# Attention and two dense layers on one core: equal blocks of tokens, and the first batch's attention moved ahead of the first product

## The chip, the cores and the metric

One core of a Trainium2 chip runs the whole program. The metric is the time of the execution on the device in microseconds (us); the median of three runs of the kernel before is 1441.01 us (1440.41 to 1442.49). TensorE (PE) multiplies, VectorE (DVE), ScalarE (ACT) and GpSimd (POOL) do the elementwise work, and SyncE (SP) issues every DMA.

## What is computed

```
k_p, v_p = mean of k, v over groups of 8 keys               # 8 batches, 8 heads, 576 tokens, 64 wide; 72 pooled keys
x = softmax(q @ k_p.T / 8) @ v_p                            # 4608 tokens x 512
h = x @ w_in;   g = where(h > 0, h, exp(min(h, 0)) - 1)     # 512 -> 2048
x1 = g @ w_out                                              # 2048 -> 512
h2 = x1 @ w_in2;  solu = h2 * softmax(h2)                   # 512 -> 1024
out = layernorm(solu) * g_ln @ w_out2                       # 1024 -> 512
```

The weights come as 64-bit floats, everything else as 32-bit floats.

## The kernel before

**Numbers.** Each product is done as three matmuls in a reduced 32-bit type: an operand is split into a high part (a cast, on ACT) and a low part (the rest, on DVE or POOL), and high x high, low x high and high x low are summed. So every first product of 128 columns of weights with a block is 12 matmuls (`m_h1`, L459) and every second one 12 more (`m_o1`, L492).

**Attention** works in units of a batch and a pair of heads: `att_setup` pools k and v, `att_S` makes scores, maxima, differences and exponentials, `att_soft` normalizes, `att_T` transposes, `att_V` multiplies by the pooled values and `att_x` writes the high and low parts of x (`xh`, `xl`). After the first batch a unit is four steps of `att_half`.

**Blocks.** The tokens are cut into blocks of 320, 256, seven of 512 and one of 448 (`sizes`). The first batch of 576 tokens is the first two blocks: its attention is split into units of 320 tokens and units of 256. The units of 320 are done in `startup`, before the first product, in an order written out by hand; those of 256 lie in block 0. The first phase then goes over slots (block `j`, 128 columns `f` of the 2048): the first product, exp, the ELU (`m_elu`, `m_glo`), the split of 128 rows of `w_out`, the second product of the slot before. A credit decides how many steps of attention go into each half slot: `need[j + 1]` is the step by which the next block's x is done.

**Weights.** In block 0 each slot also loads and converts two chunks of 128 (`conv_load`, `conv`): one pass of ACT (L400) and three bit operations of DVE (L402, L404, L406) over 1024 columns, then the split (`conv_split`, with the low part on POOL at L423). The raw 64-bit chunks, the blocks of x and the x1 on its way out share six buffers, tag `x`; wide weights and the loads of the first batch share eight, tag `w`. In the last block five slots convert the second phase's weights in the same way.

**Second phase.** 36 tiles of 128 tokens: h2, softmax and layernorm, transposes, product with `w_out2`.

**Order.** Each engine runs its own queue in order. Queues are filled by a scheduler that ranks instructions by the program's order and a model of their costs; `startup` alone is recorded as written. A tile's buffer is reused when its last reader is done, and the issue of a load into it waits on SP for that, with all later loads behind it.

Of the kernel before, what the change touches and what calls it, by code (L numbers as in the profile page):

```python
# [18 lines left out]
def kernel(  # L19
# [25 lines left out]
    SPLIT = 320  # L45
    NEXP = 12
    HS = S // 2
# [40 lines left out]

    st = {}

    def has_setup(i):
        return i == 0 or units[i][:2] != units[i - 1][:2]

    def att_load(i, what="kqv"):
        b, p, u = units[i]
        c, co = (slice(0, S), 0) if b else (slice(SPLIT, S), 0) if u else (slice(0, 384), 0)
        if i < NP:
            if ("kv", p) not in st:
                kv = sb.tile([P, 4, 512], F32, name=f"kv{i}", tag="w", bufs=8)
                kv = kv.rearrange("p a f -> p (a f)")  # L100
                n = S + P * POOL
                st["kv", p] = (kv[:, 0:S], kv[0:SK, S:n].rearrange("s (c t) -> s c t", t=POOL), kv[:, n:n + 384])
            k_t, v_t, q_t = st["kv", p]
        else:
            if i >= 2 * NP:
                k_t = sb.tile([P, S], F32, name=f"k{i}", tag="k", bufs=1)
                v_t = sb.tile([SK, P, POOL], F32, name=f"v{i}", tag="v", bufs=1)
                st["ld", i] = (k_t, v_t)
            else:
                what = "q"  # L110
            q_t = sb.tile([P, S], F32, name=f"q{i}", tag="q")
            q_t = q_t[:, c]
        if "k" in what:
            nc.sync.dma_start(out=k_t, in_=kT[b, p])
        if "q" in what:
            nc.sync.dma_start(out=q_t, in_=qT[b, p, :, c])
# [4 lines left out]
    nset = [0]  # L121
# [8 lines left out]
    def att_setup(i, what="kv"):  # L130
        b, p, u = units[i]
        early = i < NP
        if early:
            k_t, v_t, _ = st["kv", p]
# [6 lines left out]
        elif i < 2 * NP:  # L141
            return
        else:
            k_t, v_t = st.pop(("ld", i))
            kp = kpbd[nset[0] % 2]
            nset[0] += 1
# [16 lines left out]
    def att_S0(i):  # L163

        if i % 2 == 0:
            st["s0"] = ps.tile([P, 2, 512], F32, name=f"s{i}", tag="A")
        s = st["s0"]
        kp, vt = st["kp", 0, units[i][1]]
        q_t = st.pop(("q", i))
        for t in range(3):  # L170
            nc.tensor.matmul(
                s[:, i % 2, t * 2 * SK:(t + 1) * 2 * SK], q_t[:, t * P:(t + 1) * P], kp, start=True, stop=True
            )

    def att_soft0(i0):

        s = st["s0"]
        n = 6 * SK
        sv = s[:, :, 0:n].rearrange("p a (g k) -> p a g k", k=SK)
        if i0 == 0:  # L180
            st["es"] = xtile("es", F32).rearrange("p a f -> p (a f)")
        es = st["es"][:, i0 * n:(i0 + 2) * n].rearrange("p (a g k) -> p a g k", a=2, k=SK)
        mx = sb.tile([P, 2, 6, 1], F32, name=f"mx{i0}", tag="mx", bufs=4)
        sm = sb.tile([P, 2, 6, 1], F32, name=f"sm{i0}", tag="mx", bufs=4)
        nc.vector.tensor_reduce(mx[:, :, :, 0], sv, axis=AX, op=ALU.max)
        yield
        nc.vector.tensor_tensor(es, sv, mx.to_broadcast([P, 2, 6, SK]), op=ALU.subtract)
        yield
        nc.scalar.activation(es, es, AF.Exp, scale=1.0 / (8 * POOL))
        yield  # L190
        nc.vector.tensor_reduce(sm[:, :, :, 0], es, axis=AX, op=ALU.add)
        nc.vector.tensor_scalar(sm, sm, 1e-9, None, op0=ALU.add)
        nc.vector.reciprocal(sm, sm)
        yield
        nc.vector.tensor_tensor(es, es, sm.to_broadcast([P, 2, 6, SK]), op=ALU.mult)
        for a in range(2):
            st["a", i0 + a] = (es[:, a], st["kp", 0, units[i0 + a][1]][1], 6, None)
        yield

    def att_S(i):  # L200
        b, p, u = units[i]
        kp, vt = st["kp", b, p]
        q_t = st.pop(("q", i))
        tiles = QT[u]
        n = 2 * len(tiles)
        es = sb.tile([P, 10, SK], F32, name=f"es{i}", tag="es")
        mx = sb.tile([P, 10], F32, name=f"mx{i}", tag="mx", bufs=4)
        sm = None
        for t0 in range(0, len(tiles), 3):
            ts = tiles[t0:t0 + 3]  # L210
            m = 2 * len(ts)
            s = ps.tile([P, 512], F32, name=f"s{i}_{t0}", tag="C")
# [4 lines left out]
            sv = s[:, 0:m * SK].rearrange("p (a k) -> p a k", k=SK)  # L217
# [563 lines left out]
```

## Time and profile before

| | |
|---|---|
| median of the runs | 1441.01 us |
| the profiled execution | 1445.27 us |
| its span | 1443.1 us |
| PE busy | 1384.8 us (96%) |
| DVE, ACT, POOL busy | 796.6, 609.1, 333.0 us |
| bytes moved by DMA | 83.06 MB |

The span runs from the first to the last instruction of the program. A matmul's busy time overlaps that of the next one, so PE's progress is read from the time between starts, and busy shares from the union. "PEclk" in the tables of stretches is the granted share of PE's full clock. In rows of a timeline the bracket tells how long the engine stood idle before and what ended the wait.

### The profile page before, as it was taken

The numbers are of one execution on the slowest core, as the hardware profiler recorded it, in microseconds if no ns is written. First come the engines' busy times: TensorE is split into PE (matmuls) and PEld (weight loads), VectorE is DVE, ScalarE is ACT, GpSimd is POOL, SyncE is SP. The second block draws the span as 40 slices with busy tenths as digits, with TensorE's granted clock in tenths as the row PEclk, the third lists the DMA queues.
The fourth block names the chain that finished last, engine by engine and source line by source line (L and its number), as shares of the span: only waits on it lengthen the run. The fifth ranks groups of instructions, "written<-read, shape, count | busy, mean of one in ns | idle before, by whom it ended". The sixth has DMA issues, their size and how long they took to land.

```text
span 1443.1 us, 17607 instructions
## 1 busy us (share of the span) xinstructions
PE 1384.8 (96%) x6752; PEld 1134.5 (79%) x6752; DVE 796.6 (55%) x1357; ACT 609.1 (42%) x1260; POOL 333.0 (23%) x269
## 2 busy tenths in 40 slices
PE   4878999999999999999999999999999999999998
PEld 2667888787887878878788788778888888888886
DVE  5898665555465554555554333675744444455442
ACT  2555654444344444444443433444533333333332
POOL 4454433223232232322323222331000000000000
PEclk9998999999999999999999999999999999999999
DMA  6543221121121111111010010512201110110000
GB/s 211 170 158 129 68 64 42 33 64 33 33 70 34 40 56 34 42 63 42 17 46 1 8 51 0 175 59 84 74 22 51 52 52 22 52 52 22 23 22 30
DMA packets 41876, 83.06 MB, mean 58 GB/s; under 512 B 4160, under 2 KB 14912, under 8 KB 41792
## 3 DMA queue, kind: packets, MB, share of 16 engines
q1 hardware_dynamic: 41792, 81.94, 17.4%
q8 instruction: 53, 0.87, 0.2%
q14 instruction: 31, 0.25, 0.1%
HBM read 63.05 MB, written 18.87 MB: 57 GB/s over the span
## 4 chain that ended last, share of the span: by engine, by line
PE 86%; DVE 7%; ACT 2%; issue 2%; POOL 1%; DMA 1%; SPq 0%; ACTq 0%; DVEq 0%; POOLq 0%
PE h L459 25%; PE o L492 25%; PE po L577 14%; PE h L533 13%; PE s L214 2%; PE pv L300 2%; PE pt L562 2%; PE pt L261 2%; DVE cv L406 1%; DVE cv L404 1%; DMA kv<-in_v 1%; PE pv L310 0%; DVE e L470 0%; DVE wo L404 0%; PE pr L266 0%
## 5 line engine op out<-in xcount | busy, mean ns | idle before, releaser
L442 POOL TENSOR_TENSOR wol<-wo,woh 128x512 fp32r<-128x512 f32 x160 | 223.5, 1397 | 536.5 <-ACT woh L441 534.5
L459 PE MATMUL h<-xh,wh 128*128 128x512 f32 (+3 forms) x640 | 251.2, 392 | 3.4 <-DVE e L471 2.2
L459 PE MATMUL h<-xh,wl 128*128 128x512 f32 (+3 forms) x640 | 239.6, 374 | 5.8 <-POOL wl L423 5.8
L492 PE MATMUL o<-gh,woh 128*128 128x512 f32 (+3 forms) x640 | 240.7, 376 | 3.6 <-ACT gh L473 3.6
L459 PE MATMUL h<-xl,wh 128*128 128x512 f32 (+3 forms) x640 | 240.2, 375 | 0.0
L492 PE MATMUL o<-gh,wol 128*128 128x512 f32 (+3 forms) x640 | 237.8, 372 | 0.0
L470 DVE TENSOR_SCALAR e<-e 128x512 f32<-128x512 f32 (+3 forms) x160 | 72.9, 456 | 259.1 <-ACT e L464 258.8
L577 PE MATMUL po<-wh,dhl 128*128 128x512 f32 x576 | 187.3, 396 | 1.6 <-ACT dhl L565 1.6
L464 ACT ACTIVATE e<-h 128x512 f32<-128x512 f32 (+3 forms) x160 | 88.8, 555 | 229.5 <-PE h L459 227.9
L473 ACT CAST gh<-e 128x512 fp32r<-128x512 f32 (+3 forms) x160 | 92.6, 578 | 149.8 <-DVE e L471 149.8
L459 PEld LDWEIGHTS h<-xh,wh 128*128 128x128 f32 x640 | 123.0, 192 | 33.7 <-issue 12.9
L492 PEld LDWEIGHTS o<-gh,woh 128*128 128x128 f32 x640 | 122.5, 191 | 24.6 <-ACT gh L473 4.9
L459 PEld LDWEIGHTS h<-xh,wl 128*128 128x128 f32 x640 | 123.1, 192 | 23.7 <-POOL wl L423 7.4
L492 PEld LDWEIGHTS o<-gh,wol 128*128 128x128 f32 x640 | 122.6, 192 | 20.5
L459 PEld LDWEIGHTS h<-xl,wh 128*128 128x128 f32 x640 | 122.6, 192 | 20.1
L577 PEld LDWEIGHTS po<-wh,dhl 128*128 128x128 f32 x576 | 107.9, 188 | 28.5 <-ACT dhl L565 2.1
L441 ACT CAST woh<-wo 128x512 fp32r<-128x512 f32 x160 | 99.2, 621 | 66.8 <-PE o L492 59.4
L533 PE MATMUL h<-wh,x1h 128*128 128x512 f32 x288 | 115.2, 400 | 0.8 <-DVE x1s L504 0.5
L577 PE MATMUL po<-wl,dhl 128*128 128x512 f32 x288 | 113.8, 395 | 0.0
L552 POOL TENSOR_TENSOR sc<-sc,mhalf 128x1 f32<-128x1 f32 x36 | 19.7, 548 | 407.0 <-DVE sc L551 407.0
L542 ACT ACTIVATE e<-h,sc 128x1024 f32<-128x1024 f32 x36 | 40.2, 1116 | 173.6 <-DVE sc L541 173.6
L533 PE MATMUL h<-wl,x1h 128*128 128x512 f32 x288 | 112.7, 391 | 0.0
(586 smaller groups left out, 2200.1 us busy)
## 6 DMA issues: line engine op xcount, KB each, us to landing
raw<-in_w SPq DMA_DIRECT2D x48, 512.0 KB
x1r<-x1d SPq DMA_DIRECT2D x9, 1024.0 KB
out<-ot SPq DMA_DIRECT2D x36, 256.0 KB
k<-in_k SPq DMA_DIRECT2D x28, 288.0 KB
v<-in_v SPq DMA_DIRECT2D x28, 288.0 KB
q<-in_q SPq DMA_DIRECT2D x28, 288.0 KB
x1d<-x1s SPq DMA_DIRECT2D x7, 1024.0 KB
kv<-in_k SPq DMA_DIRECT2D x4, 288.0 KB
```

Source lines behind the costliest of these rows:

```text
L214: nc.tensor.matmul(s[:, t * 2 * SK:(t + 1) * 2 * SK], q_t[:, o:o + P], kp, start=True, stop=True)
L261: nc.tensor.transpose(pt[0:SK, t * P:(t + 1) * P], es[:, 2 * t + h, :], ident)
L441: nc.scalar.copy(oh, t[:, f % 4, :])
L442: nc.gpsimd.tensor_tensor(ol, t[:, f % 4, :], oh.bitcast(F32), op=ALU.subtract)
L459: nc.tensor.matmul(h[:, 0:n], a[g][:, kk, fo:fo + P], x[j][:, kk, 0:n], start=(i == 0), stop=(i == 3 * KDM - 1))
L464: nc.scalar.activation(e[:, 0:n], h[:, 0:n], AF.Exp)
L470: nc.vector.tensor_scalar(e[:, 0:n], e[:, 0:n], 1.0, 1.0, op0=ALU.min, op1=ALU.subtract)
L473: nc.scalar.copy(gh[:, 0:n], e[:, 0:n])
L492: nc.tensor.matmul(acc, a[:, dm * P:(dm + 1) * P], x[:, 0:n], start=(f == 0 and m == 0), stop=(f == NF - 1 and m == 2))
L533: nc.tensor.matmul(h[:, g, :], a[c][:, kk, o:o + P], w[g][:, kk, :], start=(m == 0), stop=(m == 3 * KDM - 1))
L542: nc.scalar.activation(e, hv, AF.Exp, bias=sc[:, 0:1], accum_out=sc[:, 1:2])
L577: nc.tensor.matmul(po, a[:, c, :], w[c // 4][:, c % 4, :], start=(m == 0), stop=(m == 3 * NC2 - 1))
```

## The change

Blocks are nine of 512 tokens. Units are whole: a batch and a pair, 576 tokens. The four units of the first batch are done in `startup`, with scores and values in the double banks (tag `A`) and the product with the reciprocals on DVE; their k and q lie in `w` buffers, their v in two `wo` buffers. `att_V` cuts the values where a block ends (512 and 64 tokens, 448 and 128, ...), not in halves of 288. The 128 tokens of batch 1 that belong to block 2 are kept in a tile `late` and split in the second slot of block 1 (`att_late`). k and v of unit 4 are pooled ahead of the loop, and block 0 takes its steps of attention (batch 1) at the rate of the other blocks, not at 0.75 a half slot.

```diff
-    sizes = [SPLIT, S - SPLIT]
-    while sum(sizes) < NT:
-        sizes.append(min(512, NT - sum(sizes)))
-    starts = [sum(sizes[:j]) for j in range(len(sizes))]
-    NBLK = len(sizes)
-
-    units = [(0, p, 0) for p in range(NP)] + [(0, p, 1) for p in range(NP)]
-
-    units += [(b, p, 2) for b in range(1, NB) for p in range(NP)]
+    NBLK = NT // 512
+    sizes = [512] * NBLK
+    starts = [512 * j for j in range(NBLK)]
+    units = [(b, p) for b in range(NB) for p in range(NP)]
     NU = len(units)
-    QT = {0: (0, P, 2 * P), 1: (0, P), 2: (0, P, 2 * P, 3 * P, S - P)}
+    QT = (0, P, 2 * P, 3 * P, S - P)
...
+        eng = nc.vector if i < NP else nc.gpsimd
+        eng.tensor_tensor(es, es, bc(sm, NG), op=ALU.mult)
...
+        j = b * S // 512
+        n = 512 * (j + 1) - b * S
+        st["pv", i] = []
+        for o, w, blk, at in ((0, n, j, b * S - 512 * j), (n, S - n, j + 1, 0)):
+            pv = next(banks)
+            for h in range(2):
+                d = slice(64 * h, 64 * h + 64)
+                nc.tensor.matmul(pv[d, 0:w], vt[:, d], a[:, h, o:o + w], start=True, stop=True)
+            st["pv", i].append((pv[:, 0:w], blk, slice(at, at + w)))
...
+            if blk == 2 and units[i][0] == 1:
+
+                if "late" not in st:
+                    st["late"] = sb.tile([P, 4, 2 * S - 1024], F32, name="late", tag="late", bufs=1)
+                nc.scalar.copy(st["late"][:, p, :], pv)
+                continue
...
+        K(0)
+        S_(0)
+        K(1)
+        S_(1)
+        M(0)
+        K(2)
+        M(1)
+        S_(2)
+        K(3)
+        att_soft(0)
+        T(0)
+        M(2)
+        S_(3)
+        att_soft(1)
+        T(1)
+        M(3)
+        V(0)
         next(ci)
+        att_soft(2)
+        T(2)
+        V(1)
+        att_x(0)
...
+        for i in range(NP):
+            att_load(i, "kq")
+        att_load(0, "v")
+        att_load(1, "v")
         conv_load(("i", 0))
+        att_load(2, "v")
+        att_load(3, "v")
         conv_load(("o", 0))
         startup()
...
+    att_setup(NP)
 
     slots = [(j, f) for j in range(NBLK) for f in range(NF)]
     for si, (j, f) in enumerate(slots):
         if f == 0:
             credit = 0.0
-            rate = 0.75 if j == 0 else max(need[j + 1] - step if j + 1 < NBLK else 0, 0) / (2.0 * NF)
+            rate = max(need[j + 1] - step if j + 1 < NBLK else 0, 0) / (2.0 * NF)
```

In `startup`, K, S_, M, V and T are the pooling of k, the scores, the maxima with the exponential, the pooling of v with the value product, and the transposes of a pair.

On DVE in the startup, before, the softmax of two pairs (`es`) alternates with the conversion of the first weights (`cv`):

```order
L191 TENSOR_REDUCE sm_129<-es 128x12
L192 TENSOR_SCALAR sm_129<-sm_129 128x12
L193 RECIPROCAL sm_129<-sm_129 128x12
L195 TENSOR_TENSOR es<-es,sm_129 128x864
L404 SCALAR_TENSOR_TENSOR cv<-raw,cv 128x1024
L185 TENSOR_REDUCE mx_162<-s_136 128x12
L187 TENSOR_TENSOR es<-s_136,mx_162 128x864
L406 SCALAR_TENSOR_TENSOR cv<-raw,cv 128x1024
```

On DVE at the same place now, `es_131`, `es_154` and `es_193` are the pairs 1, 2 and 3 of the first batch, and `k_346`, `k_352`, `k_399` the loads of k of units 4, 5 and 6:

```order
L200 TENSOR_TENSOR es_131<-es_131,sm_194 128x720
L134 TENSOR_REDUCE kr_359<-k_346 128x72
L175 TENSOR_REDUCE mx_216<-at_187 128x6
L184 TENSOR_TENSOR es_193<-at_187,mx_216 128x432
L175 TENSOR_REDUCE mx_216<-at_187 128x4
L184 TENSOR_TENSOR es_193<-at_187,mx_216 128x288
L196 TENSOR_REDUCE sm_234<-es_154 128x10
L197 TENSOR_SCALAR sm_234<-sm_234 128x10
L198 RECIPROCAL sm_234<-sm_234 128x10
L134 TENSOR_REDUCE kr_542<-k_352 128x72
L200 TENSOR_TENSOR es_154<-es_154,sm_234 128x720
L134 TENSOR_REDUCE kr_740<-k_399 128x72
```

The conversion moved behind these rows, and three reductions of batch 1's k moved in among the softmax of pairs 1 to 3.

On ACT, before, around the first exponential of the ELU (`e<-h`), one pass over raw weights (L400) stands ahead of the last cast of x:

```order
L286 COPY a_v<-pt_1_248 72x320
L400 ACTIVATE wo<-raw 128x1024
L321 CAST xh_194<-pv_254 128x320
L464 ACTIVATE e<-h_268 128x320
L441 CAST woh<-wo 128x512 x2
```

On ACT at the same place now, where `xh_266` is block 0's x and `xh_270` block 1's:

```order
L247 CAST xh_266<-at_328 128x512
L144 ACTIVATE vt_358<-vr_363 72x128
L341 ACTIVATE cv<-raw 128x1024
L247 CAST xh_270<-at_328 128x64
L341 ACTIVATE wo<-raw 128x1024
L405 ACTIVATE e<-h_366 128x512
```

The two passes over raw weights (now L341) moved between the last cast of block 0's x and the first exponential.

On POOL now, the low part of the first weights (`wl`) stands ahead of the adds over v of pair 3 (the last three of `v_92`); before it stood ahead of those of pairs 2 and 3:

```order
L113 TENSOR_TENSOR v_92<-v_92 72x128x4
L113 TENSOR_TENSOR v_92<-v_92 72x128x2
L115 TENSOR_TENSOR vr_302<-v_92 72x128
L364 TENSOR_TENSOR wl<-cv,wh 128x4x128 x2
L113 TENSOR_TENSOR v_92<-v_92 72x128x4
L113 TENSOR_TENSOR v_92<-v_92 72x128x2
L115 TENSOR_TENSOR vr_323<-v_92 72x128
```

Only pair 3 still follows the weights there, and its adds begin when the casts of the first weights are done.

## Rows read from the trace of the kernel before

**Rows 1.** Busy time by stage: stretch, its length, each engine, clock, DMA share, GB/s
```profile
0.00:42.80 42.80, 21.32 (x68) 11.93 (x68) 24.07 (x35) 13.67 (x26) 15.71 (x23) 1.00 0.63 190
42.80:142.40 99.60, 79.35 (x438) 70.29 (x438) 93.55 (x123) 56.54 (x155) 51.24 (x35) 0.90 0.49 160
142.40:207.00 64.60, 62.90 (x488) 56.84 (x486) 43.00 (x91) 40.42 (x139) 26.97 (x21) 1.00 0.21 62
207.00:308.40 101.40, 101.40 (x498) 81.66 (x497) 56.02 (x98) 44.24 (x91) 27.85 (x21) 1.00 0.13 41
308.40:411.10 102.70, 102.70 (x498) 82.41 (x496) 55.88 (x98) 44.66 (x91) 27.82 (x21) 1.00 0.15 45
820.70:908.90 88.20, 88.20 (x386) 72.20 (x385) 30.43 (x53) 30.38 (x51) 20.42 (x16) 1.00 0.07 24
908.90:1005.60 96.70, 87.74 (x397) 76.74 (x395) 68.73 (x83) 45.43 (x74) 33.69 (x20) 0.95 0.31 109
1005.60:1443.10 437.50, 431.60 (x2016) 354.00 (x2016) 209.03 (x398) 158.92 (x287) 19.74 (x36) 1.00 0.11 41
```
**Rows 2.** DVE's busy time in block 0 at L402, L404, L406, L470, L471, L480
```profile
42.80:142.40 99.60, 11.32 (x13) 0.90 0.49 160
...
42.80:142.40 99.60, 21.19 (x13) 0.90 0.49 160
...
42.80:142.40 99.60, 19.64 (x15) 0.90 0.49 160
...
42.80:142.40 99.60, 8.58 (x16) 0.90 0.49 160
...
42.80:142.40 99.60, 7.09 (x15) 0.90 0.49 160
...
42.80:142.40 99.60, 14.57 (x15) 0.90 0.49 160
```
**Rows 3.** Timeline of the startup: start, length, engine, line, operation, wait before it
```profile
1.24 0.57 SPq L114 DMA_DIRECT2D kv<-in_k  x1
...
4.57 0.75 DVE L150 TENSOR_REDUCE kr<-kv 128x72 f32<-128x576 f32 x1 [3.10 <-DMA kv<-in_k]
...
5.36 0.19 DVE L152 COPY kz<-kr 64x72 f32<-64x72 f32 x1
...
10.60 1.06 DVE L185 TENSOR_REDUCE mx<-s 128x12 f32<-128x864 f32 x1
...
17.91 2.65 POOL L126 TENSOR_TENSOR kv<-kv 72x512 f32<-72x512 f32 x2 [16.28 <-DMA kv<-in_v]
...
18.04 2.05 DVE L195 TENSOR_TENSOR es<-es,sm 128x864 f32<-128x864 f32 x1
...
23.62 1.29 DVE L406 SCALAR_TENSOR_TENSOR cv<-raw,cv 128x1024 uint32<-128x1024 uint32 x1
...
31.61 1.27 DVE L195 TENSOR_TENSOR es<-es,sm 128x864 f32<-128x864 f32 x1
```
**Rows 4.** Group of L471 at 512 columns: busy us, mean ns, idle before
```profile
L471 DVE TENSOR_TENSOR e<-e,h 128x512 f32<-128x512 f32 x112 | 77.0, 688 | 3.1
```
**Rows 5.** Timeline around the first products and of one weight load
```profile
42.50 0.42 ACT L321 CAST xh<-pv 128x320 fp32r<-128x320 f32 x1 [1.76 <-PE pv L310]
...
49.82 0.42 PE L492 MATMUL o<-gh,woh 128*128 128x320 f32 x1
...
95.27 0.81 SPq L384 DMA_DIRECT2D raw<-in_w  x2
...
100.97 1.12 ACT L400 ACTIVATE wo<-raw 128x1024 f32<-128x1024 f32 x1
```
**Rows 6.** Block 9: DVE at L402; one group of matmuls on the chain
```profile
908.90:1005.60 96.70, 7.42 (x7) 0.95 0.31 109
...
991.55 2.44 PE h L459 x12
```
**Rows 7.** Chain of waits: the first twelve matmuls of block 0
```profile
43.25 3.21 PE h L459 x12
```

More of the change, by code (lines that the diff above doesn't have):

```diff
@@ L161, in att_setup @@
         st["kp", b, p] = (kp, vt)
[L163 to L168, printed above, removed]
-        q_t = st.pop(("q", i))
[L170 to L212, printed above, removed]
+    def bc(x, m):
+        return x.rearrange("p (a o) -> p a o", o=1).to_broadcast([P, m, SK])
@@ L213, in att_S, with att_scores @@
+    def att_scores(i, banks):
+        kp, vt = st["kp", units[i][0], units[i][1]]
+        q_t = st.pop(("q", i))
+        st["sv", i] = []
+        for t0 in (0, 3):
+            s = next(banks)
+            ts = QT[t0:t0 + 3]
             for t, o in enumerate(ts):
@@ L235, in att_S, with att_exp @@
-        if i >= NEXP:
-            nc.scalar.activation(es[:, 0:n, :], es[:, 0:n, :], AF.Exp, scale=1.0 / (8 * POOL))
-        st["a", i] = (es, vt, n, sm)
+                nc.vector.tensor_tensor(es[:, g0:g0 + m, :], sv, bc(mxs, m), op=ALU.subtract)
+    def att_exp(i):
+        es, vt = st["a", i]
+        if ("sm", i) not in st:
+            nc.scalar.activation(es, es, AF.Exp, scale=1.0 / (8 * POOL))
     def att_soft(i):
-        es, vt, n, sm = st["a", i]
+        es, vt = st["a", i]
+        sm = st.pop(("sm", i), None)
@@ L273, in att_T @@
+            nc.vector.tensor_reduce(sm, es, axis=AX, op=ALU.add)
+        nc.vector.tensor_scalar(sm, sm, 1e-9, None, op0=ALU.add)
+        nc.vector.reciprocal(sm, sm)
+        eng = nc.vector if i < NP else nc.gpsimd
+        eng.tensor_tensor(es, es, bc(sm, NG), op=ALU.mult)
+    def att_T(i, h):
+        es, vt = st["a", i]
+        if h == 0:
+            st["aT", i] = sb.tile([SK, 2, S], F32, name=f"a{i}", tag="a")
+        a = st["aT", i]
         pt = ps.tile([P, 512], F32, name=f"pt{i}_{h}", tag="C")
-        for t in range(n // 2):
+        for t in range(4):
@@ L313, in att_x @@
[L313 to L322 removed]
+        nc.scalar.copy(a[:, h, 0:4 * P], pt[0:SK, :])
@@ new lines, in att_T, with att_V @@
+        if h == 1:
+            pr = ps.tile([P, 512], F32, name=f"pr{i}", tag="C")
+            for g in range(2):
+                nc.tensor.transpose(pr[0:SK, g * P:(g + 1) * P], es[:, 8 + g, :], ident)
+            lo = 5 * P - S
+            nc.scalar.copy(
+                a[:, :, 4 * P:S], pr[0:SK, 0:2 * P].rearrange("s (g t) -> s g t", g=2)[:, :, lo:P]
+            )
+    def att_V(i, banks):
+        b, p = units[i]
+        es, vt = st.pop(("a", i))
+        a = st.pop(("aT", i))
+        j = b * S // 512
[7 more added lines that the diff above has]
+            st["pv", i].append((pv[:, 0:w], blk, slice(at, at + w)))
@@ L324, with att_late, single, double @@
+    def att_late():
+        t = st.pop("late")
+        th, tl = (x[:, :, 0:2 * S - 1024] for x in xblk(2))
+        nc.scalar.copy(th, t)
+        nc.vector.tensor_tensor(tl, t, th.bitcast(F32), op=ALU.subtract)
+    def single():
+        while True:
+            yield ps.tile([P, 512], F32, name="at", tag="C")
+    def double():
+        t = ps.tile([P, 2, 512], F32, name="at2", tag="A")
+        yield t[:, 0]
+        yield t[:, 1]
     NSTEP = 4 * NU + 3
@@ L329, in att_half @@
         while nload[0] < min(NU, n // 4 + 3):
-            if nload[0] < 2 * NP or has_setup(nload[0]):
-                att_load(nload[0])
+            att_load(nload[0])
             nload[0] += 1
         i, r = divmod(n, 4)
-        whole = i > 0 and units[i - 1][2] == 2
+        before = NP <= i - 1
         if r == 0:
-            if i >= 1 and i - 1 >= NP and not whole:
-                att_T(i - 1, 1)
             if i < NU:
-                att_S(i)
+                for _ in att_scores(i, single()):
+                    pass
+                att_max(i)
+                att_exp(i)
         elif r == 1:
@@ L342, in att_half @@
                 att_soft(i)
-            if whole:
+            if before:
                 att_T(i - 1, 1)
         elif r == 2:
-            if i >= 1 and i - 1 >= NP:
-                att_V(i - 1)
-            if i + 1 < NU and has_setup(i + 1):
+            if before:
+                att_V(i - 1, single())
+                att_x(i - 1)
+            if i + 1 < NU:
                 att_setup(i + 1)
@@ L356 @@
     for j in range(NBLK):
-        end = starts[j] + sizes[j]
-        i = max(m for m in range(NU) if units[m][0] * S + SPLIT * (units[m][2] == 1) < end)
+        i = ((starts[j] + sizes[j] - 1) // S) * NP + NP - 1
         need.append(min(NSTEP, 4 * i + 7))
```

214 lines of the change are left out of this document (62 added, 152 removed).

## The prediction

> **What bounds the kernel now.** I read the busy table by stage first: the cuts are where the first product of each block of tokens begins. [rows 1] has, in order, the startup, block 0 (320 tokens), block 1 (256), block 2 and block 3 (512 each, with a batch of attention beside them), block 8 (512, no attention), block 9 (448) and the second phase. PE is busy in every microsecond of blocks 2 and 3 and of block 8, and in 431.6 of the 437.5 us of the second phase; nothing the change does off PE can show there. The time that can be won or lost lies in three rows: the startup (42.8 us, PE mostly without work), block 0 (99.6 us for 320 tokens, PE 79.35 at a granted clock of 0.90) and block 9 (96.7 us for 448 tokens at 0.95). Block 1 is near its own limit (62.9 of 64.6).
>
> Then I asked who is full in block 0: DVE, 93.55 of 99.6 us [rows 1]. By line [rows 2], 52 us of it is the three bit operations L402, L404, L406 that turn the 64-bit weights into floats, about 3.75 us for each pair of rows (11.3/13 + 21.2/13 + 19.6/15, which is 3.8), and 30 us is the ELU (L470, L471, L480). A conversion costs the same for a block of 320 tokens as for one of 512. So block 0 is a stretch whose length DVE sets, with too little matmul work laid beside it.
>
> **The change, part by part.** Blocks 2 to 7 with their batches of attention, 207.0 to 820.7, are 613.7 us; in the new kernel these are blocks 1 to 6, the same instructions but for the widths of the value products. Block 8 becomes block 7 (88.2) and the second phase stays (437.5). Together 1139.4 us on both sides. What differs is T, the time at which the second block starts (before: block 2, at 207.0, 576 tokens done; now: block 1, 512 tokens done), and L, the last block (96.7 before). 207.0 + 96.7 + 1139.4 is the 1443.1 us span.
>
> *Startup.* Each of four pairs now has five score tiles, not three. On DVE a pair costs: k reduced 0.75 and two copies of 0.2; maximum, difference and sum over 720 columns, 0.9 each (864 columns take 1.06); reciprocal and small ones 0.4; the product with the reciprocals 1.06 to 1.7 (864 columns took 1.27 alone and 2.05 beside a POOL add); the low parts of x, 512 and 64 columns, 0.9 (L471 takes 0.69 for 512 columns; the rest for the small one) [rows 3, 4]. That is 6.2 to 6.9, four times 27.5 at the upper end. The first conversion adds 3.4, and the scheduler has pulled in three reductions of k of batch 1 (2.2) and the first maxima of it (1.5): 34.6 us of DVE work. To it come waits: 4.6 until the first k is there. The reduction of k of unit 4 stands in DVE's queue ahead of the maxima of unit 3, and its load is the 18th on SP, behind 5.6 MB; 3.3 MB had landed when v came at 17.9 [rows 3], so I put it at 25 to 31, and DVE gets there at about 22: 3.5 us taken, up to 8. The next two k go through one buffer, each load issued only when the reduction before it has ended, and a k took 3.3 us from issue to use (1.24 to 4.57) [rows 3]: 3 us each. Sum 4.6 + 34.6 + 3.5 + 6 = 48.7: the first weights are converted at 48.7, before at 24.9 (23.62 + 1.29) [rows 3].
>
> From there: two casts of 512 columns (1.1, as one pass of 1024 at L400), two low parts on POOL (2.6, as two adds) and behind them, now, the three adds over v of pair 3 (3.5; two took 2.65), scale, value product and cast of x (2): about 9 us, so x of block 0 is whole at 57.5; before, its last cast began at 42.50 [rows 3, 5]. Between that cast and the first matmul of the second product there were 7.3 us (42.50 to 49.82); now two passes of 1.12 for the next weights stand on ACT ahead of the first exponential, so 10 us: 67.5 against 49.8 [rows 5]. The startup costs about 18 us.
>
> *Block 0.* Fifteen slots follow, each a first and a second product of 24 matmuls. PE: 88.2/16 = 5.5 us a slot without attention, and (102.7 - 88.2)/16 = 0.9 with it: 6.4 [rows 1]. DVE: 93.55 us before; 192 more columns cost L471 and L480 0.21 each (687 ns at 512 against 473) and L470 nothing, 16 times 0.42 = 6.7; attention is four whole units instead of four halves and three setups ahead, which I cost at nothing because three k reductions have left for the startup; 100.3 over 16 slots, less the share of one conversion already made, is 6.1 a slot [rows 1, 2, 4]. So the two engines are now level, where before PE was busy for 5.0 us a slot, part of it at half clock, and DVE for 5.8. If one hides the other wholly, a slot is 6.5; DVE's fill of block 0 (94%) gives 6.5 from its side too. Two level engines with two buffers between them don't hide each other wholly. The other bound is block 9, where the same conversions stand beside PE-bound work: a group of 12 matmuls there takes 2.44 us, 32 groups 78, the block 96.7, and 7 conversions began in it: 2.7 us for each [rows 1, 6]. Thirteen of these on fifteen slots make 8.8. I take 7.1, near the row of block 0, since there no weight buffer has to come free as in the last block. T = 67.5 + 15 x 7.1 = 174. The bounds are 165 and 199.
>
> The loads of weights: only two of the six x buffers are left to them, as before from the middle of block 0 on. A load issued at 95.27 was in use at 100.97 [rows 5], and a buffer comes round every two slots, 14 us: hidden. If slots fell under 6 us it would not be.
>
> *Last block.* 512 columns: 88.2 of pure work against 78, and each slot is 0.66 longer, which takes something off every stall: of 18.7 us lost I keep 15. L = 103, between 98 and 107.
>
> *Small ones.* The low parts of x in two pieces a unit instead of three save DVE and ACT work in blocks where PE is full: nothing. The copy of 128 late columns and their split in block 1 (0.7 us on each engine) likewise. If their cover fails they cost under 1 us.
>
> Sum: 174 + 103 + 1139.4 = 1416.4 against 1443.1, so 26.7 us less. The profiled execution took 1445.27 us, 4.3 over the median of 1441.01; taking the difference off the median gives 1414.
>
> **Two rules of the Trainium skill.** In block 0 the granted clock is 0.90, and the first 12 matmuls of 320 columns took 3.21 us, after a startup of scattered work; at block 8's pace per column they would take 1.7 [rows 1, 7]. TensorE: Matmul & The Clock Gate (Part 1) says that PE drops to half its clock after idling and regains it once busy; that speaks against the new hole in front of the second product, and by it an estimate is up to 5 us more for the first 24 matmuls. The trace agrees with the direction; I count none of it, since the slots that follow leave PE less idle than before.
>
> The product with the reciprocals took 2.05 us beside POOL and 1.27 alone [rows 3]. SBUF — State Buffer (Who interferes with whom) says that a DVE operation with two SBUF inputs waits out a GpSimd one that reads SBUF; by that each of the four new ones on DVE could lose a whole POOL add of 1.3 (2.65 for two), 5 us together, where my sum has 2.6 at most. The 0.78 of the row agrees with the kind, not the size.
>
> **Rivals.**
> *A conversion costs PE as much as in the last block* (2.7 us each). For: the mechanism, a DVE queue in which three bit operations stand before the next ELU, is the same, and DVE is fuller. Against: there ACT also waited for weight buffers. T = 199, total 1441.4 span, 1439 by the median: no change to a trifle faster.
>
> *DVE and PE take turns.* One mechanism: in each slot the 3.75 us of a conversion add to PE's 6.4 instead of lying beside it. T = 67.5 + 15 x 10.1 = 219, total 1459: slower by 18. It turns to a loss when a slot is over 8.9 us ((207.0 + 96.7 - 103 - 67.5)/15). Against: in block 0 of before, DVE was never stopped for long, so it ran ahead of PE.
>
> *The startup is longer than 67.5*: the load of k for unit 4 late by 8, the next two by 5 each, the first slots at the low clock. 13 to 15 us more, 1428.
>
> *Everything overlaps*: slots of 6.5 and L = 98, 1400.
>
> *The change doesn't take the slack it aims at*, because loads of weights come too late with two buffers: the slot would be the round trip of 5.7 + 1.1 + 3.75 + what DVE has queued, 12 to 14 for two slots, so 6 to 7: no price of its own.
>
> **How the numbers follow.** The forecast, slots of 6.8 to 7.8 and the startup within 6 us, holds 0.55 (1408 to 1426); everything overlaps 0.13; longer startup 0.17; conversions as in the last block 0.07; turns 0.08. A change of 0.2%, 3 us, is what the measurement can tell. Faster 0.87, within 0.2% 0.05, slower 0.08. The range runs from 1401 to 1434.
>
> **What would show it.** The first product of block 0 begins at 49 to 52 and the second near 67; block 1's first product at 165 to 185; DVE and PE both over 85% busy between; granted clock of that stretch over 0.95; six blocks of 102.7 after it, one of 88.2, the last at 98 to 107. A second product later than 75, or slots over 8, make the forecast wrong; so does DVE idle in block 0 for weights that haven't landed.

## The result, and the profile after

The changed kernel takes 1415.99 us (median of 4 runs, 1414.27 to 1419.41) where the kernel before took 1441.24 beside it (4 runs). The ratio is 0.983, with an interval of 0.981 to 0.985: 25 us faster. The forecast was 1414, between 1401 and 1434.

The busy table by stage, of the changed kernel, answers to [rows 1]: stretch, its length, busy time of PE, weight loads, DVE, ACT and POOL, granted clock, share of the DMA engines, GB/s.

```profile
0.00:46.20 46.20, 25.48 (x114) 18.40 (x114) 31.52 (x59) 15.03 (x34) 8.41 (x18) 0.74 0.59 170
46.20:61.20 15.00, 9.02 (x32) 5.58 (x32) 10.53 (x15) 9.62 (x34) 4.76 (x5) 0.79 0.37 122
61.20:174.80 113.60, 102.46 (x461) 77.16 (x461) 107.76 (x125) 66.10 (x164) 58.21 (x36) 0.95 0.47 155
174.80:277.50 102.70, 102.70 (x498) 82.36 (x496) 55.90 (x94) 44.18 (x88) 27.77 (x21) 1.00 0.16 45
277.50:380.30 102.80, 102.80 (x499) 82.44 (x497) 55.61 (x94) 44.19 (x87) 27.89 (x21) 1.00 0.15 45
790.10:878.40 88.30, 88.30 (x387) 72.24 (x386) 30.34 (x52) 30.39 (x50) 20.46 (x16) 1.00 0.07 24
878.40:982.00 103.60, 95.94 (x397) 75.85 (x395) 70.55 (x83) 47.80 (x74) 33.99 (x20) 0.97 0.29 102
982.00:1413.90 431.90, 425.98 (x2016) 353.94 (x2016) 209.08 (x398) 158.88 (x287) 19.73 (x36) 1.00 0.12 42
```

Block 0 begins with its first product at 46.2 and ends at 174.8; its second product begins at 61.2. From there PE and DVE are both nearly full, DVE more so. Six blocks of 512 follow, of which the table has two, then the one without attention, the last one and the second phase. Side by side, in us of the span:

| | before | forecast | after |
|---|---|---|---|
| first second-product begins | 49.8 | 67.5 | 61.2 |
| its 15 slots | | 7.1 each | 7.57 each |
| second block of 512 begins (T) | 207.0 | 174 | 174.8 |
| six blocks with attention | 613.7 | 613.7 | 615.3 |
| block without | 88.2 | 88.2 | 88.3 |
| last block (L) | 96.7 | 103 | 103.6 |
| second phase | 437.5 | 437.5 | 431.9 |
| span | 1443.1 | 1416.4 | 1413.9 |

The order of work gave 32.2 us at T and cost 6.9 in the last block. The 5.6 us of the second phase were in no step of mine.

DVE's lines of block 0 in the changed kernel, which answer to [rows 2]: L343, L345, L347 (bit operations), L411, L412 (ELU) and L421 (low part, gl_).

```profile
46.20:174.80 128.60, 16.61 (x15) 0.93 0.46 151
...
46.20:174.80 128.60, 23.76 (x15) 0.93 0.46 151
...
46.20:174.80 128.60, 21.34 (x15) 0.93 0.46 151
...
46.20:174.80 128.60, 8.28 (x16) 0.93 0.46 151
...
46.20:174.80 128.60, 10.87 (x16) 0.93 0.46 151
...
46.20:174.80 128.60, 19.61 (x16) 0.93 0.46 151
```

These are means of 1.11, 1.58, 1.42, 0.52, 0.68 and 1.23 us. The timeline of the first microseconds shows what lies in them: the same operations are short when POOL is at rest and can be long when it is not (start, length, engine, line, operation, wait before it).

```profile
54.76 0.69 DVE L343 TENSOR_SCALAR cv<-cv 128x1024 uint32<-128x1024 uint32 x1 [0.54 <-ACT cv L341]
...
64.81 0.67 DVE L412 TENSOR_TENSOR e<-e,h 128x512 f32<-128x512 f32 x1
...
66.16 1.84 DVE L421 TENSOR_TENSOR gl__463<-e,gh 128x512 fp32r<-128x512 f32 x1 [0.56 <-ACT gh L414]
...
67.93 1.88 DVE L343 TENSOR_SCALAR wo<-wo 128x1024 uint32<-128x1024 uint32 x1
...
61.25 3.72 POOL L383 TENSOR_TENSOR wol<-wo,woh 128x512 fp32r<-128x512 f32 x2 [10.06 <-ACT woh L382]
...
64.93 2.52 POOL L364 TENSOR_TENSOR wl<-cv,wh 128x512 fp32r<-128x512 f32 x2
...
67.41 1.84 POOL L200 TENSOR_TENSOR es<-es,sm 128x720 f32<-128x720 f32 x1
```

L343 takes 0.69 at 54.76 with POOL idle and 1.88 at 67.93 beside an operation of POOL that ends at 69.25, 0.56 us before it does. L412, whose second input is in PSUM, stays at 0.67.

The chain of waits from 46 to 175 in the changed kernel, some of its longer pieces (start, length, what):

```profile
67.93 1.89 DVE wo L343
...
76.19 1.77 DVE gl__527 L421
...
95.85 2.17 DVE wo L345
...
127.07 2.20 DVE wo L345
...
142.44 2.22 DVE wo L347
...
154.62 2.97 PE h L400 x12
158.03 2.77 PE o L433 x12
```

Until 150 most of its long pieces are DVE's, and long ones of their kind; only then is it PE, at full pace, to the end of the block.

### The profile page after: what moved, and what is told of

Its sections match the earlier page's. It is cut to its first block, busy times and chain, and to the rows that moved or that the text cites. A ratio compares the mean times of both kernels' runs of the same rounds, so it can differ in the third digit from the quotient of the medians.

```text
span 1413.9 us, 16571 instructions
## 1 busy us (share of the span) xinstructions
PE 1362.5 (96%) x6368; PEld 1095.4 (77%) x6368; DVE 786.6 (56%) x1280; ACT 588.6 (42%) x1149; POOL 310.8 (22%) x249
## 4 chain that ended last, share of the span: by engine, by line
PE 86%; DVE 8%; DMA 2%; issue 2%; ACT 2%; POOL 1%; SPq 0%; ACTq 0%; DVEq 0%; POOLq 0%
PE o L433 25%; PE h L400 25%; PE po L518 14%; PE h L474 14%; PE at L159 2%; PE pt L503 2%; PE at L234 2%; PE pt L210 2%; DVE cv L347 1%; DMA k<-in_k 1%; DVE wo L345 1%; DVE cv L345 1%; DVE wo L343 1%; DVE wo L347 1%; DMA raw<-in_w 1%
## 5 line engine op out<-in xcount | busy, mean ns | idle before, releaser
L383 POOL TENSOR_TENSOR wol<-wo,woh 128x512 fp32r<-128x512 f32 x144 | 206.3, 1433 | 533.9 <-ACT woh L382 533.9
L433 PE MATMUL o<-gh,woh 128*128 128x512 f32 x576 | 229.6, 399 | 9.1 <-ACT woh L382 5.0
L400 PE MATMUL h<-xh,wh 128*128 128x512 f32 x576 | 236.7, 411 | 0.5 <-ACT wh L363 0.5
L433 PE MATMUL o<-gh,wol 128*128 128x512 f32 x576 | 228.5, 397 | 1.8 <-POOL wol L383 1.8
L400 PE MATMUL h<-xl,wh 128*128 128x512 f32 x576 | 227.2, 394 | 0.0
L400 PE MATMUL h<-xh,wl 128*128 128x512 f32 x576 | 225.8, 392 | 0.7 <-POOL wl L364 0.7
L411 DVE TENSOR_SCALAR e<-e 128x512 f32<-128x512 f32 x144 | 64.7, 449 | 255.3 <-ACT e L405 255.3
L405 ACT ACTIVATE e<-h 128x512 f32<-128x512 f32 x144 | 86.0, 597 | 233.4 <-PE h L400 233.3
L414 ACT CAST gh<-e 128x512 fp32r<-128x512 f32 x144 | 89.5, 621 | 155.6 <-DVE e L412 155.6
L400 PEld LDWEIGHTS h<-xh,wh 128*128 128x128 f32 x576 | 108.7, 189 | 34.2 <-issue 13.6
L400 PEld LDWEIGHTS h<-xl,wh 128*128 128x128 f32 x576 | 108.4, 188 | 24.8
L400 PEld LDWEIGHTS h<-xh,wl 128*128 128x128 f32 x576 | 108.8, 189 | 21.9 <-POOL wl L364 1.5
L474 PE MATMUL h<-wh,x1l 128*128 128x512 f32 x288 | 112.3, 390 | 0.0
```

What stands on the lines that cost most here:

```text
L383: nc.gpsimd.tensor_tensor(ol, t[:, f % 4, :], oh.bitcast(F32), op=ALU.subtract)
L400: nc.tensor.matmul(h[:, 0:n], a[g][:, kk, fo:fo + P], x[j][:, kk, 0:n], start=(i == 0), stop=(i == 3 * KDM - 1))
L405: nc.scalar.activation(e[:, 0:n], h[:, 0:n], AF.Exp)
L411: nc.vector.tensor_scalar(e[:, 0:n], e[:, 0:n], 1.0, 1.0, op0=ALU.min, op1=ALU.subtract)
L414: nc.scalar.copy(gh[:, 0:n], e[:, 0:n])
L433: nc.tensor.matmul(acc, a[:, dm * P:(dm + 1) * P], x[:, 0:n], start=(f == 0 and m == 0), stop=(f == NF - 1 and m == 2))
```

## The experiments

My theory after the result had three parts: DVE sets the pace of block 0, the gain is a conversion's work laid beside more matmul work, and the second phase's 5.6 us are a matter of where tiles lie in SBUF. Each has rivals below. Stage times are from each kernel's profiled execution; the startup up to the first product varied from 45.8 to 48.4 us among kernels with the same startup code (the k of unit 4 landed later or earlier: DVE waited 0.45 us for it in the changed kernel and 3.05 in the one with the pad ahead of gh), so block 0 is compared from its own first product: 128.5 us in the changed kernel.

### Where the second phase's 5.6 us came from

The edit is one unused tile, here that of the first kernel; the second kernel has 8 columns of it ahead of wo and 120 behind, the third 8 ahead of gh. Bytes of a partition are worked out from the sizes and the order of the tiles in each kernel; no trace shows them.

```
             if i == 0:
+                nc.gpsimd.memset(sb.tile([P, 1528], F32, name="pad", tag="pad", bufs=1)[:, 0:8], 0.0)
             if i % 4 == 0:
                 wo[i // 4] = sb.tile([P, 4, 512], F32, name="wo", tag="wo", bufs=4)
```

> The kernel before with one unused tile of 6112 bytes a partition put ahead of the tag wo, and nothing else: the tiles that the second phase's last product loads as weights (dhl) move from byte 151424 of a partition to 157536, so that they lie at the same place modulo 8192 as the tiles it streams (o2h, o2l), as in the changed kernel. Theory 'placement': the 5.6 us by which the second phase got shorter have nothing to do with the change in the order of work; the 864 matmuls step at 227 ns, not 233, the second phase falls from 437.5 to about 432 and the time from 1441 to 1436, with block 0, block 1 and the last block as before. Rival 'spill-over': the second phase gained because the last block of 512 leaves it better off (loads landed, first conversions further); then this kernel stays at 1441 and its second phase at 437.5.

Measured: 1432.82 us against 1443.45, ratio 0.993 (0.992 to 0.994). The second phase is 432.0 long. The gain by the medians is twice what I expected: the blocks of 512 got shorter too (102.2 for 102.7, and 87.2 for 88.2). The pad had also moved gh, woh and wol, which lie behind wo.

> The changed kernel with 32 unused bytes a partition ahead of the tag wo and 480 behind it, so that dhl lies 32 bytes off, modulo 2048, from the tiles streamed against it (as in the kernel before), while the tiles of x stay where they were modulo 512. Theory 'placement': the second phase rises from 431.9 to about 437.5 and the time from 1416 to 1421.6, all earlier stages within 1 us. Rival 'spill-over', or 'an absolute place above some byte': 1416, the second phase stays at 432.

Measured: 1422.23 us, ratio to before 0.985 (0.984 to 0.987) where the changed kernel has 0.983; the second phase is 437.4, the other stages within 1.3 us of the changed kernel's.

One tile of the second phase's last product, 24 matmuls, as a piece of the chain of waits (start, length, what), in the kernel before, in the changed one and in the changed one with the 32 bytes:

```profile
1202.88 5.59 PE po L577 x24
```
```profile
1200.50 5.44 PE po L518 x24
```
```profile
1204.28 5.59 PE po L522 x24
```

The same matmuls take 5.59, 5.44 and 5.59 us a tile, and 36 tiles make 5.4 us of the 5.6. With 32 bytes in front of wo the gain is gone, whatever the order of the work: placement, not spill-over from the last block.

> The changed kernel with 32 unused bytes a partition ahead of the tag gh, so that gh, woh, wol and gl_ (streamed and weight side of the second product) all move by 32 bytes and lie at 32, not 0, modulo 64. Theory 'place modulo 64': the second product's matmuls step at 226.7 ns instead of 228.9, as they did when the pad of the kernel before moved these tiles by 6112 bytes; 1728 matmuls make 3.9 us, the blocks of 102.8 become 102.4, the time 1412. Rival 'only the place relative to the streamed tile counts' (both sides move alike here): 1416.

Measured: 1412.08 us, ratio 0.979 (0.978 to 0.981). The block without attention, of this kernel, against the 88.30 of the changed one:

```profile
789.40:876.60 87.20, 87.20 (x387) 72.19 (x386) 30.25 (x51) 30.39 (x50) 20.36 (x16) 1.00 0.07 25
```

Blocks 1 to 7 got 0.5 to 1.1 us shorter each, in a kernel in which both sides of the product moved alike: it is not only the place of one against the other.

### The parts of the change

```
-    NBLK = NT // 512
-    sizes = [512] * NBLK
+    sizes = [320, 256]
+    while sum(sizes) < NT:
+        sizes.append(min(512, NT - sum(sizes)))
...
```

The rest of the edit cuts the values at these blocks and drops the tile `late`.

> The changed kernel with the block sizes of before (320, 256, seven of 512, 448): attention of the whole first batch still stands ahead of the first product, the values are still split at the border of blocks, but the conversions lie beside a block of 320 tokens again. Theory 'a conversion needs matmul work beside it': the startup of 61 us is paid in full, and block 0 is set by DVE (15 slots of 3.75 for a conversion and 1.5 for the ELU of 320 columns, 5.3 to 5.6 us, little attention beside it): second block at 61 + 82 = 143, third at 208, last block 97, second phase 432: span about 1437, time 1434 to 1440: most of the 26 us are gone. Rival 'the whole-batch startup is what gains': then T for 576 tokens is under 190 and the time under 1420.

Measured: 1455.55 us, ratio 1.009 (1.007 to 1.010): slower than the kernel before by 13 us, where I expected 1434 to 1440. The second product begins at 62.5, block 1 at 156.2 (expected 143), block 2 at 220.7. Its block 0, whole and from the second product on:

```profile
47.80:156.20 108.40, 83.15 (x396) 71.24 (x397) 92.18 (x109) 55.05 (x129) 57.38 (x37) 0.80 0.47 155
...
62.50:156.20 93.70, 75.86 (x364) 65.91 (x365) 81.98 (x95) 45.95 (x96) 52.62 (x32) 0.80 0.49 162
```

So the rest of the change alone, with its startup, is a loss, and the larger blocks are worth 36 us on top of it by the spans (1450.1 to 1413.9), 40 by the medians. What I had wrong is the slot of 320 columns: 6.25 us and not 5.5. It was not DVE's work, which is what I had expected: 81.98/15 = 5.5 us a slot. DVE stood idle for 11.7 of the 93.7 us, and the granted clock of PE was 0.80 on the mean. Why these slots are longer than DVE's work stays open; DVE alone does not set them. That the startup is paid in full was right, that block 0 gives much of it back was wrong.

### What sets the pace of block 0

```
 def m_glo(j, f):
+    eng = nc.gpsimd if j == 0 else nc.vector
-    nc.vector.tensor_tensor(g_l[:, 0:n], e[:, 0:n], gh[:, 0:n].bitcast(F32), op=ALU.subtract)
+    eng.tensor_tensor(g_l[:, 0:n], e[:, 0:n], gh[:, 0:n].bitcast(F32), op=ALU.subtract)
```

> The changed kernel, with the low part of the activations (the subtraction of 128 x 512 that makes gl_, 0.68 us on DVE) done by POOL in block 0. Theory 'DVE sets the pace of block 0': DVE is busy 107.8 of the 113.6 us from the first second-product to block 1; 16 subtractions less are 11 us less for DVE, the slots fall from 7.57 to about 6.9 us, block 1 begins at 165 instead of 174.8, the time is 1406. Rival 'DVE and PE wait for each other in turns through the chain exp, ELU, cast, low part': POOL needs 1.26 us for what DVE does in 0.68 and has the low parts of the weights queued ahead, so the chain grows by as much as DVE gains: T within 3 us of 174.8, 1414 to 1418. Rival 'POOL is next': POOL's 58 us become 78 and the second product waits for gl_: slower than 1418.

Measured: 1430.09 us, ratio 0.991 (0.990 to 0.992): 14 us slower than the changed kernel. Block 0 is 142.1 long. Its stretch, and DVE there at L345 and L347:

```profile
47.20:189.30 142.10, 116.65 (x493) 86.05 (x493) 112.58 (x123) 76.24 (x197) 89.88 (x56) 0.92 0.42 136
...
47.20:189.30 142.10, 27.92 (x15) 0.92 0.42 136
...
47.20:189.30 142.10, 25.67 (x15) 0.92 0.42 136
```

DVE had 19.6 us less to do at L421, but its busy time fell by 5.7 only: the bit operations went from 23.76 and 21.34 to 27.92 and 25.67, and POOL took 1.82 us on the mean (29.15 for 16), and up to 2.27, for a subtraction for which DVE takes 0.68 alone. My expectation treated DVE's time as a sum of fixed durations; that falls with this run. The rival "POOL is next" gave the right sign. DVE can still be what sets the pace, but what fills it is not its own work alone.

```
 def w_out_split(f):
-    nc.gpsimd.tensor_tensor(ol, t[:, f % 4, :], oh.bitcast(F32), op=ALU.subtract)
+    nc.scalar.copy(ol, t[:, f % 4, :])
```

> The changed kernel with wol written by a copy on ACT instead of the subtraction on POOL, so that the low part of the second product's weights holds the weight itself and not its remainder: it takes 29.6 us of work (17 of 1.74) off POOL in block 0 and gives ACT about 10. Theory 'DVE loses time beside POOL': the bit operations of 1024 columns return from 2.0 and 1.6 us towards 1.22, which they take alone, DVE loses 6 to 12 of its 107.8 us in block 0 and block 1 begins at 164 to 170, 1406 to 1412. Rival 'the long ones are long for another reason': DVE is as busy as before and block 1 begins at 173 to 176, 1414 to 1418; dearer if ACT becomes the one that is waited for.

This kernel leaves out the remainder of the second product's weights. Measured: 1399.44 us, ratio 0.971 (0.969 to 0.972), below the expected 1406 to 1412, which had nothing for the last block. Block 0 is 120.1 long, 8.4 less, and the last block 96.0, 7.6 less. Block 0, and DVE at L345 and L421:

```profile
45.80:165.90 120.10, 109.06 (x492) 81.51 (x492) 100.94 (x139) 84.15 (x214) 32.77 (x24) 0.97 0.49 162
...
45.80:165.90 120.10, 20.69 (x15) 0.97 0.49 162
...
45.80:165.90 120.10, 13.41 (x16) 0.97 0.49 162
```

DVE had exactly the same instructions as in the changed kernel and 17.4 us less busy time. That is the time it lost beside POOL's 30 us of wol. L412 has 10.87 and 10.85 us in the two kernels. SBUF — State Buffer (Who interferes with whom) in the Trainium skill states that a DVE operation with two SBUF inputs contends for a shared port with a GpSimd operation that reads SBUF, that a tensor_scalar can do so too when it runs in a two-port mode, that the one that comes second waits for the whole other one, and that a DVE operation with at most one SBUF input does not contend outside these modes. The trace agrees: L345 and L421, with two SBUF inputs, gained 3.1 and 6.2 us, and L412, with one, none.

This suggests a kernel that leaves nothing out: wol on DVE, where it takes 0.68, in the two blocks where DVE is on the chain. The pad ahead of gh is in it too.

```
 def w_out_split(f, j):
+    eng = nc.vector if j in (0, NBLK - 1) else nc.gpsimd
+    eng.tensor_tensor(ol, t[:, f % 4, :], oh.bitcast(F32), op=ALU.subtract)
```

> The changed kernel with the 32-byte pad ahead of gh, and with wol (the low part of the second product's weights) subtracted on DVE instead of POOL in block 0 and in the last block; nothing is left out of the computation. Theory 'DVE operations that read SBUF stretch beside POOL': DVE takes 16 x 0.68 = 10.9 us more work and gets back the 17.7 us by which its bit operations and low parts were shorter when POOL had no wol to do, so block 0 from the first second-product to block 1 falls from 113.5 to 107 to 111 us; the last block, where the same stretch sits in the chain of the ELU, falls from 102.5 to 97 to 99; the pad gives 4. Sum 1403 to 1406. Rival 'DVE's plain load counts': 10.9 us more of DVE in a stretch that DVE fills make block 0 longer, 120 us or more, and the time is 1416 or above.

Measured: 1400.80 us, ratio 0.970 (0.969 to 0.972): 15 us faster than the changed kernel, 41 faster than the kernel before, and better than the expected 1403 to 1406. Block 0, with wol's line (L384) on DVE, and the last block:

```profile
45.90:167.60 121.70, 108.50 (x493) 82.19 (x493) 113.22 (x155) 75.71 (x197) 37.25 (x25) 0.96 0.49 160
...
45.90:167.60 121.70, 10.82 (x16) 0.96 0.49 160
...
867.50:967.10 99.60, 94.28 (x397) 75.25 (x395) 73.21 (x99) 47.28 (x74) 10.59 (x4) 0.97 0.30 106
```

DVE does 10.82 us more in block 0 and is busy 5 us less. The block is 6.8 us shorter and the last one 4.0, about 1 of that the pad's, which gives the rest in the other blocks. The rival, that DVE's plain load counts, is out.

### The startup and the clock

```
+        for m in range(12):      # 28 in the second kernel
+            nc.tensor.matmul(o1[0][1][:, 1, :], wh[0][:, 0, 0:P], xh[0][:, 3, :], start=True, stop=True)
```

> The changed kernel with 12 extra matmuls of 512 columns on PE, between the second first-product and the first second-product of block 0, into a PSUM bank that the second product then overwrites from the start; they fill the hole of 5.0 us in which PE waits for the first woh, after which the trace shows the half clock until 68.5. Theory 'DVE sets the pace': the first second-product runs at 0.23 us a matmul instead of 0.43 and ends some 3 us earlier, but block 1 still begins at 174 to 176 and the time stays at 1416, because DVE has been busy without a break since 53. Rival 'the clock gate cost the 0.47 us by which a slot was longer than forecast': block 1 begins 4 to 6 us earlier, near 170, 1411.

Measured: 1414.51 us, ratio 0.980 (0.978 to 0.982). The 12 matmuls ended 2.3 us before the first woh was there, and the granted clock fell to half all the same. Block 0 took 126.8 us and block 1 began at 173.5, between what the theory (174 to 176) and the rival (near 170) had said. Inconclusive on the clock; so a longer one:

> As the earlier kernel with extra matmuls ahead of the first second-product, with 28 of them instead of 12: the 12 ran in 2.9 us at full clock, left 2.3 us of the hole open, and the half clock came all the same (61.7 to 68.5). 28 take 6.4 us at full clock, from 56.5 to 63, so PE is not without work before the first wol is there at about 64. Theory 'DVE sets the pace, the clock costs nothing': the first second-product runs at 0.23 us a matmul, ends near 67 instead of 68.5, and block 1 still begins at 173 to 175.5, 1414 to 1416. Rival 'the half clock is part of what a slot lost': block 1 begins 2 to 4 us earlier, at 170.5 to 172.5, 1411 to 1413.

Measured: 1414.93 us, ratio 0.982 (0.980 to 0.983). The first matmul of the second product in this kernel, and the stretch that compares with 61.20:174.80 above:

```profile
67.20 0.39 PE L433 MATMUL o<-gh,woh 128*128 128x512 f32 x1
...
61.20:174.80 113.60, 103.86 (x480) 80.34 (x478) 108.39 (x128) 66.78 (x165) 58.31 (x35) 0.98 0.47 155
```

The clock was full through the second product and 0.98 in the stretch instead of 0.95, and block 0 took 128.3 us, like the 128.5 of the changed kernel. But the half clock had moved rather than gone: it lies from 53.5 to 60.0 here, in the first product, whose matmuls step at 0.43 us there. And the extra matmuls ran until 67.2. Counted from the block's first product, the second product began 4.3 us later than in the changed kernel (19.3 and 15.0) and ended as late as before (22.1 and 22.4); I had expected it to end earlier. The run shows that a second product that begins 4.3 us later, at full clock, costs nothing. What the half clock costs it doesn't separate. An upper bound from the changed kernel's rows, from the second product on: the 12 matmuls step at 0.43 us where they step at 0.23 at full clock, 2.4 us, and a later stretch at half clock, 102.7 to 106.1, had PE busy for 3.1 us, so 1.5 more. A stretch ahead of that, 48.2 to 51.2 in the first product, cost nothing: PE stood idle for 0.57 us behind it, until ACT's kz for the next value product was there.

```
         att_soft(3)
+        next(co)
         T(3)
+        next(co)
+        next(co)
         att_x(1)
...
         att_x(2)
+        next(co)
         V(3)
         att_x(3)
-        for _ in co:
-            pass
```

> The changed kernel with the conversion of the first pair of second-product weights moved up in the startup, into stretches where DVE waits (3.4 us at 39, 2.9 us at 48.7) and ACT has 5.6 us without work; their load has landed at 22. Theory 'DVE sets the pace from 53 on': 3.1 us of DVE work and one ACT pass leave the full stretch, the second product begins at 57 to 58 instead of 61.2 and block 1 at 171 to 172: 1412 to 1413. Rival 'something else sets block 0' (weights landing, PE at half clock): the second product begins earlier, but block 1 still at 174 to 175, 1416.

Measured: 1416.06 us, ratio 0.982 (0.981 to 0.983): no change. The second product began at 64.4, later than 61.2. POOL's adds over v of the fourth pair, in this kernel and in the changed one:

```profile
49.67 2.94 POOL L113 TENSOR_TENSOR v<-v 72x512 f32<-72x512 f32 x2
```
```profile
48.73 1.98 POOL L113 TENSOR_TENSOR v<-v 72x512 f32<-72x512 f32 x2
```

DVE's sign operation at 49.5 now stood beside them and they took 1 us more; another came from a startup 0.9 us later, and the last full cast of x began at 55.0 instead of 52.9. What DVE had gained it lost again in waiting for x. Neither my theory nor its rival had that.

```
         V(2)
+        att_setup(3, "v")
         next(ci)
...
-        V(3)
+        att_V(3, double())
```

> As the kernel with wol on DVE and the pad, and with the three POOL adds over v of the fourth pair issued ahead of the low parts of the first weights (wl), no longer behind them. Theory 'the fourth pair's v gates x of block 0': in the changed kernel POOL waited 12.4 us for wh, then did wl, then these adds until 51.2; now they are done before 44, the last cast of x ends near 50 instead of 53.5, the first group of 12 matmuls 3 us earlier, and block 1 begins 1 to 4 us earlier than without this edit. Rival 'DVE is full from 53 on anyway': block 1 begins at the same time within 1 us.

Measured: 1399.05 us, ratio 0.970 (0.968 to 0.972). The second product begins at 58.0, and block 0 falls from 121.7 to 118.4, but its startup was 2.5 us longer (2.2 of it waits for the three k), so block 1 begins at 166.8 against 167.6: within the 1 us that the rival had said. Against the kernel without the edit the times overlap: by the length of block 0 it is likely worth 2 to 3 us, not shown.

The last kernel puts this edit and that of the moved conversion together.

> As the kernel before in this list (wol on DVE, pad, v of the fourth pair early), and with the conversion of the first pair of second-product weights moved into the startup's holes as well. With the adds over v out of the way, the conversion no longer stands beside them on DVE: the second product begins at 55 to 58 and block 1 begins 2 to 4 us earlier than without this edit, 1397 to 1401 in all. Rival 'as when it was tried alone': the second product begins no earlier, since the chain exp, ELU, cast and the first wol set it, and the time is the same within 1 us.

Measured: 1401.98 us, ratio 0.973 (0.970 to 0.975). Block 0 is 124.1 long and begins its second product at 59.4: no gain, the expected 2 to 4 us did not come. DVE was idle for 9.0 us of the stretch from the second product on (112.6 long, 103.59 busy), where it was idle for 1.7 without the moved conversion (108.8 and 107.12); why was not followed up.

## Why the prediction was right, point by point

The sum came out within 2 us of the median because the two large terms, T and L, were right to 1 us. For T that is luck: inside it a startup 6.3 us too long and fifteen slots 7.1 us too short cancelled. And one term outside was missed. By the profiled executions the gain is 29.2 us, by the medians 25.3; the forecast of 26.7 lies between, since the profiled execution of before was 4 us above its median.

*Startup, 6.3 us too long.* I charged 9.5 us of waits for the three k that the scheduler had pulled in; DVE waited 0.45 and 1.30 for them, as these rows of the changed kernel's timeline show, and not at all for the one between.

```profile
23.78 0.75 DVE L134 TENSOR_REDUCE kr<-k 128x72 f32<-128x576 f32 x1 [0.45 <-DMA k<-in_k]
...
31.45 0.75 DVE L134 TENSOR_REDUCE kr<-k 128x72 f32<-128x576 f32 x1 [1.30 <-DMA k<-in_k]
...
42.48 0.69 DVE L248 TENSOR_TENSOR xl<-at,xh 128x512 fp32r<-128x512 f32 x1 [3.37 <-ACT xh L247]
...
52.91 0.58 ACT L247 CAST xh<-at 128x512 fp32r<-128x512 f32 x1
...
61.23 0.80 PE L433 MATMUL o<-gh,woh 128*128 128x512 f32 x1 [5.04 <-ACT woh L382]
```

In other kernels with this startup the first of these waits was up to 3.05 us, so part of the error differs from execution to execution. Part of the gain came back as waits for ACT's casts (3.37 here), which I had not in the sum. The first weights were ready at 45.5 and not 48.7, the last full cast of x began at 52.9, and from it to the second product there were 8.3 us and not 10. That the adds over v of the fourth pair stand behind wl was right: POOL did them from 48.7 to 51.2.

*Block 0, 0.47 us a slot too short.* The failed step is "6.1 a slot" for DVE: it was 107.76/15 = 7.2, or 118.3 us in the whole block (the 10.53 of the second row with it) where 16 times 6.1 are 98. Two more conversions fell into the block than before (15 at L343 and L345 for 13: 5.4 us), where I had deducted one (2.7), the reduction over v came twice as often (3.6), and the bit operations at L343 and L347 stretched further than before (1.11 and 1.42 us for 0.87 and 1.31: 5.3). That is 17.0 of the 20.7 us; the rest was not traced. I had counted the attention of the block at nothing, one conversion less and not two more, and took durations from the trace as if they belonged to the operation. That the two engines would not hide each other wholly, at 7.1 against 6.5, was right in kind; about half of what stands between 6.5 and 7.57 is POOL's wol (15 slots of 7.0 us without it on POOL), and at most the rest is the two buffers, which no run here tests.

*The last block* was 103.6 against 103. Its stalls, which I left as they were, have in part the same cause: it took 96.0 with wol copied on ACT and 97.0 to 99.8 in the three kernels with wol on DVE and the pad. Some 2 us of such a difference can be something else, since kernels that have the changed kernel's last block unaltered took 101.3 (granted clock 1.00) to 103.6 (0.95).

*The second phase*, counted at no change, gave 5.6 us by a move of tiles in SBUF that the diff doesn't show: the tag wo is first used earlier, so it is laid out ahead of x. The two kernels with a pad ahead of wo show that the place does it. Without it the span would have been 1419.5, and the forecast 3 us too low.

*The two rules.* The low clock came as weighed, at the lower of PE's two levels (1.2 of 2.4 GHz), from 58.3, when PE had been idle since 56.2, to 68.5:

```profile
58.30:68.50 10.20, 5.51 (x12) 4.03 (x13) 9.64 (x12) 4.88 (x8) 7.25 (x5) 0.50 0.64 200
```

TensorE: Matmul & The Clock Gate (Part 1) in the Trainium skill has the clock fall to half after idling, and the trace agrees. I had counted nothing for it; its price is between nothing and the 3.9 us of the bound above, and no run here parts the two. The shared port I had priced in the wrong place: the four products on DVE in the startup lost 0.8 us together (three took 0.91, one 1.73), under my 2.6, while block 0 held the 17.4 us. A good part of such a loss lay in the 93.55 us of before already, whose bit operations were nearly as long (0.87, 1.63 and 1.31 us on the mean, where alone they take 0.69 and 1.22).

*The rivals.* "Conversions as in the last block" (8.8 a slot) and "turns" (10.1) didn't happen, nor did "everything overlaps" (6.5). Of the signs I named, T, the blocks, L and both engines' 85% (DVE 118.29 and PE 111.48 of 128.6) came in; the first product was earlier than 49, the second earlier than 67, and the clock of the stretch was 0.93 and not over 0.95. DVE was idle for 5.8 of 113.6 us, so weights that had not landed can have cost no more than that.

## What to carry to other kernels

A fixed cost on one engine that goes with each block (here the conversions) is best laid beside the largest block: the loss at the start was 12 us, the gain from equal blocks of 512, the first two merged, 36 or more. The busy time of DVE is not its load: look whether the same operation has two durations in the trace and what POOL does during the long one, before work is moved to POOL. When a diff changes which tag is used first, compare the stages that it doesn't touch; a gain there may be the place in SBUF.

## What the chip showed that was not expected

Matmuls of 512 columns depend on where their tiles begin in SBUF. With dhl at byte 0 modulo 64 of a partition and the streamed weights at 32, the 24 matmuls of a tile of the last product took 5.59 us, with both at 32 they took 5.44. With gh, woh and wol at 0 the block without attention took 88.3, at 32 87.2. The pads of 32 and of 6112 bytes moved the time alike, and the 32 bytes that undo the place undid the gain. Other offsets were not tried, so the modulus is a guess from these, and why 32 is better than 0 stays open.

The stretch beside each other works both ways: a subtraction of 512 columns took POOL 1.28 us alone (the first wol of the kernel with the moved conversion), 1.74 on the mean in block 0 of the changed kernel and 1.82 for gl_ when that was on POOL. What a piece of work costs on either engine is so not a number of its own.
